# Retention and an MLP on one core: small matmuls in quarters of the array, one stretch for two chunks, and a new order of the head

## The chip, the core and the metric

One NeuronCore of a Trainium2 chip runs one program. The metric is the device time in microseconds (us) of the whole program. TensorE (PE in the profile; PEld are its weight loads) does the matmuls, VectorE (DVE), ScalarE (ACT) and GpSimd (POOL) the element-wise work. SP and POOL issue most of the transfers (DMA). SBUF is the working memory of 128 partitions; matmuls write to PSUM, 8 banks of 512 float32 per partition.

## The reference

q, k and v have shape (8, 8, 576, 64): batch, heads, positions, head width.

```
scores = q @ k.T / sqrt(64)
ret    = scores * D[h]              # D[h][i, j] = gamma_h ** (i - j) for i >= j, else 0
x      = (ret @ v), heads side by side    # 4608 tokens x 512
h      = x @ w_in                   # 512 x 2048
out    = (h * tanh(softplus(h))) @ w_out  # Mish, then 2048 x 512
```

## The kernel before

**Chunks.** Each batch's 576 positions are cut into chunks of 128, the last one of 64; the last ones of two batches share a chunk (c = 4). There are 36 chunks, in `chunks` (L52 to L57): first the eight first chunks (c = 0), then per pair of batches the rest. Four chunks make a tile of 512 tokens, nine tiles in all. Since gamma^(i-j) splits into a factor of i and one of j, a chunk's retention is the causally masked product within the chunk plus q times a running state, the sum of k^T v over earlier chunks.

**Steps of a chunk** (n from 8 on; `N0` = 8):
- `load` (L253): q, k and v by POOL's queue; k is cast to bf16 on the way.
- P (`step_p`, L271, DVE) and V (`step_v`, L276, POOL) scale q and v by the factors of position and head.
- T (`step_t`, L282) transposes q and k: for n < 18 (`NPE`) by eight matmuls against the identity and one ACT copy, later by a transposing transfer on SP's queue (L291).
- S (`step_s`, L294): scores of 8 heads, transposed; a head has 64 rows, so two heads lie in the two row halves of the array (eight pairs of 128-column matmuls), and DVE masks the result into `sm`.
- `state(upto)` (L319) computes at most one more state, if chunk `upto` still lacks its own: eight matmuls add k^T v of one chunk to the PSUM bank `st`; DVE copies it out as `ssb`, doubled in width, with zeros in the half that belongs to the other head (`diag`).
- O (`step_o`, L343): eight matmuls of the state with q and eight of v with `sm`, all with 128 rows and 64 columns of the array, into one bank; DVE copies it to `xT`.

**MLP.** `g1` (L366) makes one of 16 slices of h for a tile: four matmuls over 512 columns into bank `hp`, then Mish on ACT into `gT`. `g2` (L375) does a quarter of 128 output tokens: four matmuls over 512 columns into `ops` (sometimes `hp`); each fourth call readies a result, which `stores` copies (DVE) and SP stores.

**Order.** All orders are written out by hand; each engine and each queue executes its own in order. In the steady loop (L563), tile t runs 16 steps i of g1(t, i) and g2(t-1, i), and a visit of eight steps (w = i % 8) handles two chunks n, n+1 of the next tile: at w = 0 a state if needed and S of n and n+1; at w = 4 a state, O of both, a state; V of n+2, n+3 at w = 0 and 1; T of n+2, n+3 at w = 0, 1 (by TensorE at w = 5, 6, with P at 1, 3); P of n+4, n+5 at w = 7; loads at w = 4, 5. Tile 1's g1 and its first g2 stand in a loop of 24 steps u (L529) in which chunks 8 to 13 come one by one: P and V at u = 4j, S, states and O at 4j + 1, T at 4j + 3.

**Head.** Tile 0 holds the first chunks of batches 0 to 3, which need no state. q comes by SP's queue (L119), the rest by POOL's: k, v of batches 0 and 1 (`load_first_v(0)`, L142), the first quarter of w_in (L143), v of batches 2 and 3 (L144), the other quarters. The v are cast by `f_v` (L220), on POOL for the first three, DVE for the fourth. `f_scores`, `f_out` (L225) do the products; `keep_warm` (L164) issues matmuls on zeros while TensorE would wait. G1 of tile 0 begins with its first four slices on the columns of batches 0 and 1 only (`half`), then, after `f_out` of 2 and 3, on the other columns, and then goes on with whole slices (L495).

**Layout.** Partition 64 e + d of `xT`, group p, holds head 2p + e; w_in's rows (c p) are loaded in the same order, one transfer of 128 partitions for each quarter.

Of the kernel before, what the change touches and what calls it, by code (L numbers as in the profile page):

```python
# [17 lines left out]
def kernel(  # L18
# [63 lines left out]
    w_in_r = moe_w_in.rearrange("(c p) f -> p c f", p=P)  # L82
    w_out_r = moe_w_out.rearrange("(f p) d -> p f d", p=P)

    def load_w_in(f0, n):
        nc.gpsimd.dma_start(out=w_in_t[:, :, ds(f0, n)], in_=w_in_r[:, :, ds(f0, n)])
# [55 lines left out]
    load_first_v(0)  # L142
    load_w_in(0, 512)  # L143
    load_first_v(2)  # L144
# [13 lines left out]

    diag = consts.tile([P, 2], F32)
    nc.vector.memset(diag, 0.0)  # L160
    nc.vector.memset(diag[0:64, 0:1], 1.0)
    nc.vector.memset(diag[64:P, 1:2], 1.0)
# [62 lines left out]
    def f_out(t, b, copy):  # L225
        if b == 0:
            xts[t] = xp.tile([P, KC, NCH * P], BF16, name="xT")
        vb = fst[t]["vb"][b]
        if t == 0:
            pool, name = ((ps_h, "hp"), (ps_h, "hp"), (ps_st, "st"), (ps_o, "ops"))[b]  # L230
            ot = pool.tile([P, NP, P], F32, name=name)
        else:
            ot = ps_sc.tile([P, 2, NP, P], F32, name="sc")[:, 0]
        for p in range(NP):
            for e in range(2):
                nc.tensor.matmul(ot[ds(64 * e, 64), p, :], lhsT=vb[:, 2 * p + e, :],
                                 rhs=fst[t]["sm", b][:, 2 * p + e, :],
                                 start=(p == 0), stop=True, skip_group_check=True)
        copy(xts[t][:, :, ts(b, P)], ot)  # L239
# [54 lines left out]
    def step_s(n):  # L294
        b, c = chunks[n]
        qk = live[n]["qk"]
        sc = ps_sc.tile([P, 2, NP, P], F32, name="sc")
        for p in range(NP):
            for e in range(2):
                r = ds(64 * e, 64)  # L300
                nc.tensor.matmul(sc[:, e, p, :], lhsT=qk[r, 1, p, :], rhs=qk[r, 0, p, :],  # L301
                                 start=True, stop=True)
        sm = tr.tile([P, 2, NP, P], BF16, name="sm", bufs=3)
        m = mask if c < 4 else mask2
        nc.vector.tensor_tensor(  # L305
            sm.rearrange("p e n i -> p (e n) i"), sc.rearrange("p e n i -> p (e n) i"),
            m.unsqueeze(1).to_broadcast([P, 2 * NP, P]), op=OP.mult)
        live[n].update(sc=sc, sm=sm)
# [10 lines left out]
    def state(upto):  # L319
# [11 lines left out]
        for p in range(NP):  # L331
# [3 lines left out]
        ssb = tr.tile([P, 2, NP, 64], BF16, name="ssb", bufs=6)  # L335
        nc.vector.tensor_tensor(  # L336
            ssb.rearrange("p e n d -> p e (n d)"),
            st.rearrange("p n d -> p (n d)").unsqueeze(1).to_broadcast([P, 2, NP * 64]),
            diag.unsqueeze(2).to_broadcast([P, 2, NP * 64]), op=OP.mult)
# [3 lines left out]
    def step_o(n):  # L343
        b, c = chunks[n]
        t, s = divmod(n, NCH)
        assert done[0] > state_of[n]
        qk, vs, sc, sm = (live[n][x] for x in ("qk", "vs", "sc", "sm"))
        ot = ps_o.tile([P, NP, P], F32, name="ops") if t == 2 else sc[:, 0]
        halves = [(0, P, b, c - 1)] if c < 4 else [(0, 64, b, 3), (64, 64, b + 1, 3)]
        for i0, iw, bb, cc in halves:  # L350
            for p in range(NP):
                for e in range(2):
                    nc.tensor.matmul(ot[ds(64 * e, 64), p, ds(i0, iw)], lhsT=st_sb[bb, cc][:, e, p, :],  # L353
                                     rhs=qk[:, 0, p, ds(i0, iw)],
                                     start=(i0 == 0 and p == 0), stop=False, skip_group_check=True)
        for p in range(NP):
            for e in range(2):
                nc.tensor.matmul(ot[ds(64 * e, 64), p, :], lhsT=vs[:, 2 * p + e, :], rhs=sm[:, e, p, :],  # L358
                                 start=False, stop=True, skip_group_check=True)
        if s == 0:  # L360
            xts[t] = xp.tile([P, KC, NCH * P], BF16, name="xT")
        nc.vector.tensor_copy(xts[t][:, :, ts(s, P)], ot)  # L362
# [3 lines left out]
    def g1(t, f, cols=slice(0, NCH * P)):  # L366
# [3 lines left out]
        for c in range(KC):  # L370
            nc.tensor.matmul(hp[:, cols], lhsT=w_in_t[:, c, ts(f, P)], rhs=xts[t][:, c, cols],  # L371
                             start=(c == 0), stop=(c == KC - 1))
        nc.scalar.activation(gts[t][:, f, cols], hp[:, cols], AX.Mish)  # L373

    def g2(t, i):  # L375
# [3 lines left out]
        if part == 0:  # L379
            if (t == nT - 1 and s % 2) or (t == 1 and s < 2):  # L380
# [49 lines left out]
    def att(n, steps):  # L430
        if n >= n_chunks:
            return
        for step in steps:
            {"P": step_p, "V": step_v, "T": step_t, "S": step_s, "O": step_o}[step](n)
# [4 lines left out]
    half = (slice(0, 2 * P), slice(2 * P, 4 * P))  # L439
# [18 lines left out]
    keep_warm(3, ps_h, "hp")  # L458
    f_out(0, 0, dve)
    f_out(0, 1, act)  # L460
    f_scores(0, 1)
    f_v(0, 3, dve)
    keep_warm(3, ps_st, "st")
    for f in range(4):
        g1(0, f, half[0])
    f_out(0, 2, act)
    f_out(0, 3, dve)
    for f in range(4):
        g1(0, f, half[1])
# [25 lines left out]
    for f in range(4, nF):  # L495
        g1(0, f)
# [30 lines left out]

    att(N0, "PV")
    for u in range(24):  # L529
        j, w = divmod(u, 4)  # L530
        if w == 0 and j > 0:
            att(N0 + j, "PV")
# [7 lines left out]
        elif w == 1 and j > 0:  # L540
            if j > 3:
                state(N0 + j - 1)
            if j < 5:
                att(N0 + j - 1, "S")
            if j < 4:
                state(N0 + j - 1)
            if j > 1:
                att(N0 + j - 2, "O")
            if j == 4:
                state(N0 + j - 1)  # L550
            stores()
        elif w == 2 and 0 < j < 5:
            f_state(1, j - 1, nc.vector)
        elif (w == 3 and j < 5) or (w == 2 and j == 5):
            att(N0 + j, "T")
# [6 lines left out]

    for t in range(2, nT + 1):  # L563
        for i in range(nF):
            n, w = NCH * (t + 1) + i // 8 * 2, i % 8
            if t in (3, 4) and i in (4, 12):
                load_k0(2 * t - 2 + i // 8)
            by_pe = n + 2 < NPE
            if w == 0:
                stores()  # L570
                state(n + 1)
                att(n, "S")
                att(n + 1, "S")
            if w == 4:
                state(n + 3)
                stores()
                att(n, "O")
                att(n + 1, "O")
                state(n + 3)
            if by_pe and w in (1, 3):  # L580
                att(n + 2 + w // 2, "P")
            if w in (0, 1):
                att(n + 2 + w, "V")
            if w in (4, 5):
                more_loads(n + w - 2 + PF)
            if w - (5 if by_pe else 0) in (0, 1):
                att(n + 2 + (w == 1 or w == 6), "T")
            if w == 7 and n + 4 >= NPE:
                att(n + 4, "P")
                att(n + 5, "P")  # L590
            stores()
            if t < nT:
                g1(t, i)
            if t == 2:
                if i % 2:
                    g2(1, 8 + i // 2)
            elif t < nT or i < 12:
# [33 lines left out]
```

## Time and profile before

| | us |
|---|---|
| three runs | 312.32, 312.5, 315.58 |
| median | 312.5 |
| the profiled execution, its time | 313.61 |
| its span, first to last instruction | 311.9 |
| TensorE busy / VectorE / ScalarE / GpSimd in that span | 300.3 / 137.1 / 110.7 / 143.6 |
| TensorE busy in 0 to 20 us / 80 to 260 us | 13.7 of 20 / 178.8 of 180 |
| mean of a 512-column matmul from start to modelled end | 0.38 |
| granted TensorE clock | 1.00 |

A line of the timeline gives the start, the time from the first start to the last end, the engine, the source line, the operation, what it writes and reads, the rows * columns of the array that it uses, shape and type of the moving operand, how many instructions are merged, and in brackets how long the engine stood idle ahead of it and what released it. Matmuls overlap: the distance from start to start tells what one costs. In groups, the figures behind the bar are busy us, mean ns of one, idle us ahead of them. 42.85 MB move in the span; the mean busy share of the transfer engines is nine tenths or more in nearly every slice until 160 us.

### The profile page before, as it was taken

What the parts mean: (1) busy time and instruction counts of PE and PEld (TensorE: products, weight loads), DVE (VectorE), ACT (ScalarE), POOL (GpSimd) and SP (SyncE); (2) the same over time, 40 slices, a digit from 0 to 9 for tenths busy, and PEclk for the clock granted to TensorE, in tenths of its full rate; (3) what the DMA queues carried; (4) which work ended last, traced back from release to release, by engine and by line L of the source; (5) the groups of instructions that cost most, each with busy time, mean ns of one, the idle gap of its engine ahead of it and who ended that gap; (6) DMA issues with size and microseconds to landing.
All of it is one profiled execution on the core that took longest, in us unless ns stands there. A gap on an engine that the chain in (4) does not pass through costs nothing.

```text
span 311.9 us, 5809 instructions
## 1 busy us (share of the span) xinstructions
PE 300.3 (96%) x2429; PEld 152.3 (49%) x2468; DVE 137.1 (44%) x200; ACT 110.7 (36%) x183; POOL 143.6 (46%) x178
## 2 busy tenths in 40 slices
PE   7769999999999999999999999999999999999995
PEld 3444554555465554545454444545454544444444
DVE  4723455778637635443434453535354332001111
ACT  4546345671453623233333333232323333333300
POOL 8578849989985976274726262612010000000000
PEclk9999999999999999999999999999999999999999
DMA  7999999999995999999996949371504100010031
GB/s 177 234 206 205 220 208 221 256 171 175 232 203 96 148 181 191 155 195 146 179 178 116 189 88 218 77 144 37 101 36 101 36 34 36 35 34 34 36 101 68
DMA packets 73642, 42.85 MB, mean 137 GB/s; under 512 B 58640, under 2 KB 64528, under 8 KB 73616
## 3 DMA queue, kind: packets, MB, share of 16 engines
q0 software_dynamic: 48640, 27.27, 61.1%
q1 hardware_dynamic: 24832, 15.08, 23.3%
q8 instruction: 19, 0.31, 0.5%
q10 hardware_dynamic: 144, 0.13, 0.1%
q14 instruction: 7, 0.06, 0.1%
HBM read 38.80 MB, written 9.44 MB: 155 GB/s over the span
## 4 chain that ended last, share of the span: by engine, by line
PE 92%; issue 2%; DMA 2%; POOL 2%; DVE 0%; ACT 0%; POOLq 0%; ACTq 0%
PE hp L371 39%; PE ops L386 30%; PE hp L386 4%; PE sc L301 3%; PE st L333 3%; DMA gT<-in_v_dram 2%; PE hp L403 2%; PE sc L353 2%; PE sc L358 2%; PE sc L288 1%; PE st L403 1%; PE ops L403 1%; PE hp L414 1%; POOL gT L106 1%; POOL vb L222 1%
## 5 line engine op out<-in xcount | busy, mean ns | idle before, releaser
L371 PE MATMUL hp<-xT,w_in_t 128*128 128x512 bf16 (+1 forms) x562 | 141.3, 373 | 2.2 <-DVE xT L239 0.8
L373 ACT ACTIVATE gT<-hp 128x512 bf16<-128x512 f32 (+1 forms) x148 | 86.8, 586 | 156.4 <-PE hp L371 144.2
L386 PE MATMUL ops<-w_out_t,gT 128*128 128x512 bf16 x430 | 110.1, 379 | 0.4
L371 PEld LDWEIGHTS <-w_in_t 128*128 128x128 bf16 x592 | 55.1, 98 | 61.9 <-DVE xT L239 1.3
L386 PEld LDWEIGHTS <-gT 128*128 128x128 bf16 x496 | 48.2, 98 | 58.1 <-issue 0.8
L422 DVE COPY res<-ops 128x512 f32<-128x512 f32 x28 | 19.3, 688 | 82.7 <-PE ops L386 79.7
L279 POOL TENSOR_TENSOR vs<-vraw,gv 128x512 bf16<-128x512 f32 x28 | 30.3, 1096 | 51.8 <-PE sc L358 37.6
L336 DVE TENSOR_TENSOR ssb<-st,diag 128x512 bf16<-128x512 f32 x32 | 21.9, 685 | 47.2 <-PE st L333 47.2
L305 DVE TENSOR_TENSOR sm<-sc,mask 128x1024 bf16<-128x1024 f32 x28 | 33.0, 1215 | 6.2 <-PE sc L301 6.2
L263 POOL DMA_DIRECT2D qraw<-in_q_dram x24 | 21.8, 910 | 12.8 <-DVE qks L273 9.6
L263 POOL DMA_DIRECT2D vraw<-in_v_dram x24 | 21.8, 908 | 2.9 <-DMA vpair<-in_v_dram 1.5
L263 POOL DMA_DIRECT2D qks<-in_k_dram x24 | 21.8, 906 | 1.3 <-DMA w_out_t<-in_moe_w_out_dram 0.9
L273 DVE TENSOR_TENSOR qks<-qraw,gq 128x512 bf16<-128x512 f32 x28 | 20.2, 758 | 0.0
L362 DVE CAST xT<-sc 128x512 bf16<-128x512 f32 x24 | 15.3, 680 | 0.0
L386 PE MATMUL hp<-w_out_t,gT 128*128 128x512 bf16 x61 | 14.7, 379 | 0.2
L289 ACT COPY qkT<-sc 128x1024 bf16<-128x1024 bf16 x10 | 10.1, 1010 | 8.0 <-PE sc L288 8.0
L215 DVE TENSOR_TENSOR sm<-sc,dmask 128x1024 bf16<-128x1024 f32 x8 | 9.4, 1220 | 5.0 <-PE sc L211 5.0
L353 PE MATMUL sc<-qkT,ssb 128*64 128x128 bf16 (+1 forms) x224 | 9.5, 213 | 0.0
L358 PE MATMUL sc<-sm,vs 128*64 128x128 bf16 x192 | 9.4, 219 | 0.0
L301 PE MATMUL sc<-qkT 64*128 64x128 bf16 x224 | 9.0, 218 | 0.0
L403 PEld LDWEIGHTS <-gT 128*128 128x128 bf16 x64 | 5.8, 98 | 6.5
L267 POOL DMA_DIRECT2D qraw<-in_q_dram x8 | 5.6, 706 | 7.3 <-DVE qks L273 7.3
(103 smaller groups left out, 192.0 us busy)
## 6 DMA issues: line engine op xcount, KB each, us to landing
out_dram<-res SPq DMA_DIRECT2D x31, 256.0 KB, 3.0
qraw<-in_q_dram POOLq DMA_DIRECT2D x24, 256.0 KB, 6.0
vraw<-in_v_dram POOLq DMA_DIRECT2D x24, 256.0 KB, 6.8
qks<-in_k_dram POOLq DMA_DIRECT2D x24, 128.0 KB, 6.4
w_in_t<-in_moe_w_in_dram POOLq DMA_DIRECT2D x4, 512.0 KB, 11.1
w_out_t<-in_moe_w_out_dram POOLq DMA_DIRECT2D x4, 512.0 KB, 9.8
gT<-in_q_dram SPq DMA_DIRECT2D x4, 256.0 KB, 4.9
gT<-in_k_dram POOLq DMA_DIRECT2D x8, 128.0 KB, 6.3
```

The costliest lines, as they stand in the source:

```text
L263: nc.gpsimd.dma_start(out=t, in_=src[b, :, ds(P * c, P), :].rearrange("h p d -> p h d"))
L273: nc.vector.tensor_tensor(live[n]["qks"][:, 0], live[n]["q"], gq[:, c, :].unsqueeze(2).to_broadcast([P, H, D]), op=OP.mult)
L279: nc.gpsimd.tensor_tensor(vs, live[n]["v"], gv[:, c, :].unsqueeze(2).to_broadcast([P, H, D]), op=OP.mult)
L301: nc.tensor.matmul(sc[:, e, p, :], lhsT=qk[r, 1, p, :], rhs=qk[r, 0, p, :], start=True, stop=True)
L305: nc.vector.tensor_tensor(sm.rearrange("p e n i -> p (e n) i"), sc.rearrange("p e n i -> p (e n) i"), m.unsqueeze(1).to_broadcast([P, 2 * ...
L336: nc.vector.tensor_tensor(ssb.rearrange("p e n d -> p e (n d)"), st.rearrange("p n d -> p (n d)").unsqueeze(1).to_broadcast([P, 2, NP * 64 ...
L353: nc.tensor.matmul(ot[ds(64 * e, 64), p, ds(i0, iw)], lhsT=st_sb[bb, cc][:, e, p, :], rhs=qk[:, 0, p, ds(i0, iw)], start=(i0 == 0 and p == ...
L371: nc.tensor.matmul(hp[:, cols], lhsT=w_in_t[:, c, ts(f, P)], rhs=xts[t][:, c, cols], start=(c == 0), stop=(c == KC - 1))
L373: nc.scalar.activation(gts[t][:, f, cols], hp[:, cols], AX.Mish)
L386: nc.tensor.matmul(ops, lhsT=gts[t][:, f, ts(s, P)], rhs=w_out_t[:, f, :], start=(f == 0), stop=(f == nF - 1))
L403: nc.tensor.matmul(outs[0, s], lhsT=gts[0][:, f, ts(s, P)], rhs=w_out_t[:, f, :], start=(f == 0), stop=(f == nF - 1))
L422: copy(ot, ops)
```

## The change

It has six parts.

1. Heads h and h + 4 now share a group of `xT`: partition 64 a + r of group c holds head 4a + c. w_in is loaded in that order of rows, each quarter by two transfers of 64 partitions.
2. The state is copied out as it is, without the zeros, 256 elements per partition instead of 512; in the steady loop (`two`) half by DVE, half by ACT. Its product with q (`outputs_end`) uses quarters of the array, 64 rows by 64 columns, as does S now: twice as many matmuls with half the columns.
3. O becomes `outputs` and `outputs_end` for two chunks at once, into two banks, copied to `xT` by ACT and DVE. `visit` puts state, outputs, state, outputs_end and S of the next two chunks in one stretch, at w = 6.
4. In the steady loop P moves to w = 4, 5, transposing transfers to w = 7 and the next w = 0, T on TensorE to w = 2, 4; two g1 stand together at w = 0 and 4.
5. `hold`: at w = 4 POOL copies one element of each of the two transposed chunks, so that it waits for their transfers before it issues its next loads.
6. In the head, v of batches 2 and 3 is loaded ahead of w_in; the half-width G1 is gone, and G1 starts whole after the four `f_out`; other engines take some of the copies, and the counts of `keep_warm` change. In the loop over u, P, V and T get their own lists, S and O stand at u = 9, 15 and 22.

```diff
-    w_in_r = moe_w_in.rearrange("(c p) f -> p c f", p=P)
+    w_in_r = moe_w_in.rearrange("(a c r) f -> a r c f", a=2, r=64)
-        nc.gpsimd.dma_start(out=w_in_t[:, :, ds(f0, n)], in_=w_in_r[:, :, ds(f0, n)])
+        for a in range(2):
+            nc.gpsimd.dma_start(out=w_in_t[ds(64 * a, 64), :, ds(f0, n)], in_=w_in_r[a, :, :, ds(f0, n)])
...
     load_first_v(0)
+    load_first_v(2)
     load_w_in(0, 512)
-    load_first_v(2)
...
@@ step_s
-                r = ds(64 * e, 64)
-                nc.tensor.matmul(sc[:, e, p, :], lhsT=qk[r, 1, p, :], rhs=qk[r, 0, p, :],
-                                 start=True, stop=True)
+                for a in range(2):
+                    r, j = ds(64 * e, 64), ds(64 * a, 64)
+                    nc.tensor.matmul(sc[j, e, p, :], lhsT=qk[r, 1, p, j], rhs=qk[r, 0, p, :],
+                                     start=True, stop=True, skip_group_check=True)
...
@@ state
-        ssb = tr.tile([P, 2, NP, 64], BF16, name="ssb", bufs=6)
-        nc.vector.tensor_tensor(
...
+        ssb = tr.tile([P, NP, 64], BF16, name="ssb", bufs=6)
+        if two:
+            nc.vector.tensor_copy(ssb[:, 0:2, :], st[:, 0:2, :])
+            nc.scalar.copy(ssb[:, 2:NP, :], st[:, 2:NP, :])
+        else:
+            nc.vector.tensor_copy(ssb, st)
...
+    def outputs(n, banks):
+        both = [pool.tile([P, 2, 2 * P], F32, name=name) for pool, name in banks]
+        for x in range(2):
+            sm, vs = live[n + x]["sm"], live[n + x]["vs"]
+            for h in range(NP):
+                for a in range(2):
+                    hh = NP * a + h
+                    nc.tensor.matmul(both[h % 2][ds(64 * a, 64), h // 2, ts(x, P)], lhsT=vs[:, hh, :],
+                                     rhs=sm[:, hh % 2, hh // 2, :],
+                                     start=(x == 0 and h < 2), stop=False, skip_group_check=True)
+        return both
...
+    def outputs_end(n, both):
...
+                        e, p = h % 2, (NP * a + h) // 2
+                        r = ds(64 * e, 64)
+                        nc.tensor.matmul(both[e][ds(64 * a, 64), h // 2, ds(P * x + i0, iw)],
+                                         lhsT=st_sb[bb, cc][r, p, :], rhs=qk[r, 0, p, ds(i0, iw)],
+                                         start=False, stop=True, skip_group_check=True)
...
+        for e, copy in enumerate((nc.scalar.copy, nc.vector.tensor_copy)):
+            copy(xts[t].rearrange("p (h e) i -> p e h i", e=2)[:, e, :, ds(P * s, 2 * P)], both[e])
...
+    def hold(n):
+        nc.gpsimd.tensor_copy(held[:, n % 2:n % 2 + 1], live[n]["qk"][:, 1, NP - 1, P - 1:P])
+
+    def visit(n, banks, upto, two=False):
+        state(upto, two)
+        both = outputs(n, banks)
+        state(upto, two)
+        outputs_end(n, both)
+        for m in (n + 2, n + 3):
+            att(m, "S")
...
@@ head
-    keep_warm(3, ps_h, "hp")
-    f_out(0, 0, dve)
+    keep_warm(4, ps_h, "hp")
+    f_scores(0, 1)
+    f_out(0, 0, act)
     f_out(0, 1, act)
-    f_scores(0, 1)
-    f_v(0, 3, dve)
-    keep_warm(3, ps_st, "st")
-    for f in range(4):
-        g1(0, f, half[0])
-    f_out(0, 2, act)
-    f_out(0, 3, dve)
-    for f in range(4):
-        g1(0, f, half[1])
+    keep_warm(6, ps_st, "st")
+    f_v(0, 3, act)
+    f_out(0, 2, dve)
+    f_out(0, 3, act)
+    keep_warm(2, ps_sc, "sc")
...
@@ loop over u
+    pv = {0: 0, 4: 1, 8: 2, 11: 3, 16: 4, 18: 5}
+    tp = {3: 0, 6: 1, 11: 2, 13: 3, 18: 4, 20: 5}
...
+        if u == 9:
+            state(N0 + 1)
+            att(N0, "S")
+            att(N0 + 1, "S")
+            state(N0 + 1)
+        elif u == 15:
+            visit(N0, ((ps_o, "ops"), (ps_h, "hp")), N0 + 3)
+            state(N0 + 3)
+        elif u == 22:
+            visit(N0 + 2, ((ps_h, "hp"), (ps_h, "hp")), N0 + 5)
...
@@ steady loop
+            if w == 6 and n < n_chunks:
+                visit(n, ((ps_h, "hp"), (ps_h, "hp")), min(n + 4, last), True)
                 state(n + 3)
...
+            if w in (4, 5) and n + 4 >= NPE:
+                att(n + w, "P")
...
+            if w == 4 and NPE <= n + 2 < n_chunks:
+                hold(n + 2)
+                hold(n + 3)
...
+            if w in (2, 4) and n + 2 < NPE:
+                att(n + 1 + w // 2, "T")
             if w == 7 and n + 4 >= NPE:
-                att(n + 4, "P")
-                att(n + 5, "P")
+                att(n + 4, "T")
+            if w == 0 and n + 2 >= NPE:
+                att(n + 3, "T")
```

## The prediction

> **What bounds the kernel now.** I read the page first (shares of the engines, the chain that ended last), then TensorE's timeline, stretch by stretch, then the timeline of the first 35 us, then the groups by form and the landings of the transfers. The page says which engine counts:
>
> ```profile
> span 311.9 us, 5809 instructions
> PE 300.3 (96%) x2429; PEld 152.3 (49%) x2468; DVE 137.1 (44%) x200; ACT 110.7 (36%) x183; POOL 143.6 (46%) x178
> ...
> PE 92%; issue 2%; DMA 2%; POOL 2%; DVE 0%; ACT 0%; POOLq 0%; ACTq 0%
> ```
>
> Nothing but TensorE carries the chain, so only what TensorE executes, or waits for, can move the end. Its timeline in the steady part, one visit of two chunks (16.02 us from one S stretch, 203.04, to the next, 219.06):
>
> ```profile
> 202.08 1.03 PE L386 MATMUL ops<-w_out_t,gT 128*128 128x512 bf16 x4
> 203.04 0.62 PE L301 MATMUL sc<-qkT 64*128 64x128 bf16 x16
> ...
> 204.46 1.03 PE L386 MATMUL ops<-w_out_t,gT 128*128 128x512 bf16 x4
> ...
> 209.64 1.03 PE L386 MATMUL ops<-w_out_t,gT 128*128 128x512 bf16 x4
> 210.60 0.32 PE L333 MATMUL st<-vs,qks 128*64 128x64 bf16 x8
> 210.75 0.42 PE L353 MATMUL sc<-qkT,ssb 128*64 128x64 bf16 x16
> 211.00 0.39 PE L358 MATMUL sc<-sm,vs 128*64 128x128 bf16 x8
> 211.23 0.39 PE L353 MATMUL sc<-qkT,ssb 128*64 128x128 bf16 x8
> 211.45 0.39 PE L358 MATMUL sc<-sm,vs 128*64 128x128 bf16 x8
> 211.80 0.32 PE L333 MATMUL st<-vs,qks 128*64 128x64 bf16 x8
> ...
> 212.92 1.03 PE L386 MATMUL ops<-w_out_t,gT 128*128 128x512 bf16 x4
> ```
>
> Read the starts; the durations overlap. A group of four 512-column matmuls takes 0.865 us, 0.216 each. From that: the S stretch is due at 202.08 + 0.865 = 202.945, starts 0.09 late, and the next group (0.865 before 204.46) starts at 203.595. So S is 0.65 = 0.09 to enter, 0.45 for 16 matmuls (eight pairs, one per row half), 0.10 to leave. The O stretch is due at 210.505 and over at 212.055: 1.55 = 0.09 + state 0.15 + four groups of eight in column halves (0.25 where the chunk is split, else 0.223 each) + a wait of 0.13 + state 0.15 + 0.10. The 0.13 wait: the state bank may only be written again when DVE's copy of it (0.69, start 0.24 after the last matmul's start) is through. Where a state stands ahead of S it costs 0.25, 0.10 of it for the change from column halves to row halves.
>
> ```profile
> L336 DVE TENSOR_TENSOR ssb<-st,diag 128x512 bf16<-128x512 f32 x32 | 21.9, 685 | 47.2 <-PE st L333 47.2
> L417 DVE COPY half<-hp 128x256 f32<-128x256 f32 x1 | 0.4, 424 | 2.8 <-PE hp L414 2.8
> ```
>
> Summed the same way over the trace: tile 1 (55 to 77 us) has five stretches, 0.67 + 1.12 + 1.12 + 1.44 + 0.79 = 5.1; after it twelve S (12 x 0.65, four with a state: + 4 x 0.25) 8.8 and twelve O (seven of 1.54, four of 1.44, one of 1.14) 17.7. Together 31.6 us; everything else after 20 us is 512-column matmuls (and transposes, which stay). The head:
>
> ```profile
> 7.12 1.17 POOL L117 DMA_DIRECT2D gT<-in_v_dram  x1
> ...
> 14.77 2.11 PE L371 MATMUL hp<-xT,w_in_t 128*128 128x256 bf16 x16
> ...
> 17.67 0.87 POOL L222 CAST vb<-gT 128x512 bf16<-128x512 f32 x1 [4.51 <-DMA gT<-in_v_dram]
> ...
> 18.60 0.41 PE L236 MATMUL st<-sm,vb 128*64 128x128 bf16 x8 [1.72 <-POOL vb L222]
> ...
> 20.03 12.67 PE L371 MATMUL hp<-xT,w_in_t 128*128 128x256 bf16 x63 [0.79 <-DVE xT L239]
> ...
> 32.53 0.61 PE L194 MATMUL sc<-ident,qbx 128*128 128x128 bf16 x8
> ```
>
> The second pair of v lands at 17.6 and G1 of the second half waits for it. G1 is over at 32.53. The half-width matmuls take 2.11 / 16 = 0.132 each where half of 0.216 would be 0.108.
>
> **The change, part by part.** Base: this execution, 313.61 us (span 311.9, 1.7 around it); it is 1.1 above the median of 312.5, and gains are carried to the median.
>
> *Quarters and one stretch.* A visit now runs: enter 0.09; state 0.15; sm.v of both chunks, 16 matmuls in column halves, 8 x 0.056 = 0.45; state 0.15; change of mode 0.10; state.q, 16 matmuls of 64 x 64, four quads; S of the next two chunks, 32 matmuls of 64 x 64, eight quads; leave 0.10. No row shows four quarters side by side. From below, a quad can't beat one 128-column step, 0.056 (the pair's). From above, it is two pair steps, 0.112. Between lies the rate of issue: 16 matmuls, each with its weights, in 0.25 us (210.75 to 211.00) is 0.0156 each, 0.063 a quad. Row halves and column halves both run a pair in one step, so I take the near row: 0.056, that is 0.22 and 0.45.
>
> The skill's page "TensorE: Matmul & The Clock Gate" (section "Wait — 56ns, not 53.3ns?") says that starts never come closer than about 25 ns. The 0.0156 above is already below it; by the rule 48 matmuls would take 1.2 us instead of 0.67, 0.5 a visit, some 7 us in all, and the change would lose.
>
> *The wait between the two states.* The diagonal mask goes, so the copy has 256 elements, and in the steady part half each on DVE and ACT. DVE at 512 takes 0.688 (res copy), at 256 0.424, so 128 takes about 0.29. It starts 0.24 after the last state matmul's start and frees the bank 0.14 later (211.65 to 211.80): 0.67, covered by 0.03 + 0.45. A wait of 0.19 stays, 0.11 where a new batch begins (there the row shows 0.06 to restart). So the old wait does not vanish, it grows a little, as less work stands between. Bounds: 0 and, with DVE's undivided 0.424, 0.33.
>
> *Sum of the stretches.* A visit: 1.71 + 0.19 = 1.90. Eleven with two states and S: 11 x 1.71 + 7 x 0.19 + 4 x 0.11 = 20.6; three of them need a third state after S: 3 x 0.25; the last has neither state nor S: 0.95. That is 22.3 against 26.5. Tile 1 has three stretches: u = 9 (state, S, S, state) 1.2, u = 15 2.25, u = 22 2.0: 5.45 against 5.1, since S of two more chunks falls in it. Net 31.6 - 27.75 = 3.9 us gained; with 0.063 a quad 3.2; with no wait left 5.6.
>
> *What moves to other engines.* xT of a pair is one copy on ACT (0.585) and one on DVE (0.69) instead of two on DVE; ACT also gets 22 half states. Per visit ACT is busy 4.8 of 16 us, DVE 7.2; neither is near. The copies free the two hp banks while S and the following g2 (0.45 + 0.865) run, so g1 finds a bank. In t >= 3 two g2 groups (1.7 us) stand before the visit and cover the Mish (0.60) that must free them. In tile 1 and t = 2, P stands a step ahead of T, with DVE's two sm (1.22 each) before it: T(14) comes 4.3 us after the visit, DVE needs about 3.9; close, priced at nothing.
>
> *Transposing transfers.* P and T move earlier, but S more: T to S shrinks from 15.4 and 13.6 us to 12.1 and 10.4 (seven and six steps of 1.73). The transfers land in 9.4 to 11.8 us in the first three visits (108 to 143 us, all queues full), in 3.1 to 6.9 later. So only visits 16 to 20 are at stake. `hold` makes POOL wait for them ahead of load_k0 and the loads: 18 copies of at most 0.29 (L486's row), and behind them wait six loads that nobody reads for two visits. With fewer loads beside them they should land in under 9.4. Bounds: nothing, and 3 x 4.8 = 14 (a first issue of 5.1 on SP, the longest of the rows, puts the second off by 3.4: 11.8 + 3.4 - 10.4). I take 0.5: the first has no hold ahead of it. On SP, T stands ahead of the stores, which have four buffers.
>
> *Head.* v(2) is issued at 6.4, ahead of w_in 0, so it takes the place that w_in 0 had: lands at 14.1 to 15. w_in 0 then lands when the same bytes had come, 17.0 to 17.6. Eight half issues of 0.525 (L106) to 0.756 (L86) instead of four: POOL is through w_in at 12.8 to 14.2 rather than 11.84, and the v casts behind it (0.58 each) end at 14.9 to 16.0. TensorE then has six warming matmuls (1.3) and f_out 2 and 3; with the copy (0.24 + 0.69) G1 may start at 16.6 to 18.1. I take 17.7, just behind w_in 0. 64 x 0.216 = 13.8 ends it at 31.5: 1.0 gained (0.4 to 1.6). The later w_in land at 19.8 to 24.9, each before its turn (21.2 on). From there the loads' order is the same; v of tile 1 lands at 45.06, and its products, at 48.3 instead of 49.4, still cover that.
>
> "DMA: Bandwidth & Descriptors" (section "Rules for kernel authors") says of two transfers to disjoint partition halves that they serialize, so one whole transfer is better: by it the split is pure cost. Here the layout needs it, and its issue time is above.
>
> *Sum.* 3.9 + 1.0 - 0.5 = 4.4. This execution would go to 309.2, the median to **308.1**.
>
> **Rivals.**
> - *Quads run as pairs.* 12 more steps of 0.056 a visit, 0.67, on thirteen visits, and as many for the last one's state.q and the S of u = 9 together: 14 x 0.67 = 9.4 in all, 317.5, slower. For it: no quad in this trace. Against it: either split alone runs side by side with starts 3.4 ns apart. It decides from about 0.082 a quad on, where the 4.4 are gone. A limit on dispatch would look the same: a visit has 80 matmuls where the longest stretch of before has 56.
> - *Transposes late.* Visits 16, 18 and 20 wait 1.4 each or more: from 312 up, 318 at worst likely. For it: 11.8 landed against 10.4 lead. Against: hold, and the landings of 3 to 7 us once loads are few. It costs the gain from 1.5 a visit on.
> - *The state's wait grows.* If DVE or ACT is not free when the state ends (a store's copy of 0.69 ahead of it), the wait is 0.5 rather than 0.19: 11 x 0.35 = 3.9, 312.0: nothing gained but the head. Against: DVE stood idle 4.86 us ahead of L336.
>
> **How the numbers follow.** Forecast 0.64 (own range 305.0 to 310.5: no wait left and the best head, 308.1 - 1.7 - 0.6 = 305.8, some more for the wait taken for T; 0.063 a quad and the worst head, 309.4, some more for T); pairs 0.13; late transposes 0.12; state's wait 0.08; something else 0.03. 1% of the time, 3.1 us, is about what a measurement tells from nothing, so the bounds are 309.4 and 315.6. Faster: 0.58 of the forecast's and 0.03 of others, 0.61; slower: the pairs, and 0.05 of late transposes and the rest, 0.18; within: 0.21. The range reaches from 305.0 to 313.5, up to the state's wait and most of the late transposes; beyond it are the pairs.
>
> **What would show it.** Right: one stretch of about 1.9 us each 15.7 us on TensorE, with L301's successor taking 0.056 for four; G1 starting at 17.7 and over at 31.5; a wait of about 0.2 ahead of the second state. Wrong: 32 S matmuls in 0.9 us; TensorE waiting for the transposing transfer at visits 16 to 20; G1 waiting for xT or w_in past 18.5.

## The result, and the profile after

| | before | after |
|---|---|---|
| median of the runs (four of each) | 312.52 | 317.52 |
| lowest to highest | 312.32 to 315.58 | 317.40 to 317.67 |
| profiled execution, its span | 313.61, 311.9 | 317.57, 315.9 |
| TensorE: S, state and O stretches from 55 us on | 31.6 | 31.8 |
| G1 of tile 0 over at | 32.53 | 35.18 |

The changed kernel is slower: ratio 1.0146, 95% interval 1.0101 to 1.0190. The forecast was 308.1, its range ended at 313.5.

The page of the changed kernel, to be laid beside the three lines shown of before (TensorE is 96% busy in both):

```profile
span 315.9 us, 6341 instructions
PE 301.7 (96%) x2682; PEld 150.7 (48%) x2682; DVE 118.8 (38%) x181; ACT 124.2 (39%) x217; POOL 149.0 (47%) x200
...
PEclk9979999999999999999999999999999999999999
...
PE 89%; DVE 3%; DMA 3%; POOL 2%; issue 1%; ACT 1%; DVEq 0%; POOLq 0%; ACTq 0%
```

Two things are new. The clock row (one digit for each fortieth of the span, in tenths) has a 7 in its third slice, about 16 to 24 us. And the chain that ended last now runs through VectorE (3%) and ScalarE (1%), which held 0% of it before.

The timeline of one visit, all engines (16.02 us to the next visit, as before):

```profile
202.13 0.32 PE L330 MATMUL st<-vs,qks 128*64 128x64 bf16 x8
...
202.27 0.62 PE L352 MATMUL hp<-sm,vs 128*64 128x128 bf16 x16
...
202.55 0.29 DVE L334 CAST ssb<-st 128x128 bf16<-128x128 f32 x1 [2.48 <-PE st L330]
...
202.88 0.27 ACT L335 CAST ssb<-st 128x128 bf16<-128x128 f32 x1 [1.77 <-DVE ssb L334]
...
203.19 0.32 PE L330 MATMUL st<-v0s,k 128*64 128x64 bf16 x8 [0.30 <-ACT ssb L335]
...
203.44 0.42 PE L369 MATMUL hp<-qkT,ssb 64*64 64x128 bf16 x16
...
203.69 0.62 PE L298 MATMUL sc<-qkT 64*64 64x128 bf16 x32
...
204.24 1.04 PE L414 MATMUL ops<-w_out_t,gT 128*128 128x512 bf16 x4
```

The two half copies do not run side by side. ScalarE had stood idle for 1.77 us, and what released it at 202.88 was VectorE's half. Only behind it may the second state start. From the starts: sm.v is issued through at 202.27 + 0.45 = 202.72, the second state starts at 203.19, so the wait is 0.47. The bracket says 0.30 because it counts from the modelled end. The quarters do what they should: 32 S matmuls in 204.24 - 0.10 - 203.69 = 0.45, and state.q's 16 in 0.25.

The head, from the timeline of 4 to 23 us:

```profile
14.79 0.62 POOL L87 DMA_DIRECT2D w_in_t<-in_moe_w_in_dram  x1 [1.66 <-DMA gT<-in_v_dram]
...
15.39 1.73 POOL L218 CAST vb<-gT 128x512 bf16<-128x512 f32 x3
...
16.08 0.96 PE L232 MATMUL hp<-sm,vb 128*64 128x128 bf16 x16 [2.84 <-POOL vb L218]
...
16.98 2.68 PE L163 MATMUL st<-zeros 128*128 128x512 bf16 x6
...
21.37 1.89 PE L399 MATMUL hp<-xT,w_in_t 128*128 128x512 bf16 x8
```

POOL's last issue of w_in waited 1.66 us until v of batches 2 and 3 had landed. The casts queued behind it therefore began at 15.39 (11.99 before), TensorE stood idle for 2.84 us, and the six warming matmuls took 2.68 us, where six take 1.47 at full clock (in the run with more warming matmuls below): the granted clock is 0.54 in 17 to 18 us, 0.50 from 18 to 20, and 1.00 from 21 on. G1 starts at 21.37 and is over at 35.18. The halved clock is no accident of this one execution: the four runs have mean granted clocks of 0.995, 0.995, 0.995 and 0.989, and 3.4 or 6.8 us at half clock take 0.005 or 0.011 off the mean of 316 us.

And tile 1, where one transpose was late:

```profile
71.92 2.35 DVE L302 TENSOR_TENSOR sm<-sc,mask 128x1024 bf16<-128x1024 f32 x2
...
74.52 1.82 DVE L269 TENSOR_TENSOR qks<-qraw,gq 128x512 bf16<-128x512 f32 x2
...
75.79 0.62 PE L284 MATMUL sc<-ident,qks 128*128 128x128 bf16 x8 [1.23 <-DVE qks L269]
```

T of chunk 12 was due at 74.40 and waited 1.40 us for P: VectorE had two sm and a state copy of the visit ahead of it, and the first P took 1.21 us (the second 0.68). While it ran, GpSimd ran V (74.12 to 75.17) and a transfer's issue. Over all the traces, the 159 P that had no GpSimd instruction beside them took at most 0.69 us; the longest of all, 2.94, had one beside it.

### The profile page after: what moved, and what is told of

Read it like the earlier page. It is cut to its first block, busy times and chain, and to the rows that moved or that the text cites. A ratio compares the mean times of both kernels' runs of the same rounds, so it can differ in the third digit from the quotient of the medians.

```text
span 315.9 us, 6341 instructions
## 1 busy us (share of the span) xinstructions
PE 301.7 (96%) x2682; PEld 150.7 (48%) x2682; DVE 118.8 (38%) x181; ACT 124.2 (39%) x217; POOL 149.0 (47%) x200
## 4 chain that ended last, share of the span: by engine, by line
PE 89%; DVE 3%; DMA 3%; POOL 2%; issue 1%; ACT 1%; DVEq 0%; POOLq 0%; ACTq 0%
PE hp L399 39%; PE ops L414 31%; PE st L330 3%; PE hp L414 3%; DMA gT<-in_v_dram 3%; PE hp L431 2%; PE sc L298 2%; PE sc L284 1%; PE hp L369 1%; PE st L431 1%; PE ops L431 1%; PE hp L442 1%; DVE ssb L334 1%; ACT ssb L335 1%; PE st L163 1%
## 5 line engine op out<-in xcount | busy, mean ns | idle before, releaser
L399 PE MATMUL hp<-xT,w_in_t 128*128 128x512 bf16 x576 | 136.6, 379 | 0.1
L401 ACT ACTIVATE gT<-hp 128x512 bf16<-128x512 f32 x144 | 86.1, 598 | 112.2 <-PE hp L399 112.2
L414 PEld LDWEIGHTS <-gT 128*128 128x128 bf16 x496 | 47.4, 98 | 56.0
L259 POOL DMA_DIRECT2D qraw<-in_q_dram x24 | 21.8, 907 | 3.6 <-DMA vpair<-in_v_dram 1.5
L334 DVE CAST ssb<-st 128x128 bf16<-128x128 f32 x22 | 6.4, 292 | 43.2 <-PE st L330 43.2
L335 ACT CAST ssb<-st 128x128 bf16<-128x128 f32 x22 | 5.9, 266 | 26.6 <-DVE ssb L334 26.6
L375 DVE CAST xT<-hp 128x512 bf16<-128x512 f32 x14 | 9.7, 692 | 4.5 <-PE hp L369 3.9
L330 PE MATMUL st<-vs,qks 128*64 128x64 bf16 x192 | 7.6, 200 | 2.6 <-ACT ssb L335 2.5
L330 PEld LDWEIGHTS <-qks 128*64 128x64 bf16 x192 | 5.1, 110 | 9.3 <-issue 7.6
L375 ACT CAST xT<-hp 128x512 bf16<-128x512 f32 x13 | 7.7, 591 | 4.2 <-PE hp L369 4.2
```

The source lines that it names most:

```text
L259: nc.gpsimd.dma_start(out=t, in_=src[b, :, ds(P * c, P), :].rearrange("h p d -> p h d"))
L330: nc.tensor.matmul(st[ds(64 * e, 64), p, :], lhsT=ks[:, 2 * p + e, :], rhs=vs[:, 2 * p + e, :], start=(c == 0 and p == 0), stop=True, skip ...
L375: copy(xts[t].rearrange("p (h e) i -> p e h i", e=2)[:, e, :, ds(P * s, 2 * P)], both[e])
L399: nc.tensor.matmul(hp, lhsT=w_in_t[:, c, ts(f, P)], rhs=xts[t][:, c, :], start=(c == 0), stop=(c == KC - 1))
L401: nc.scalar.activation(gts[t][:, f, :], hp, AX.Mish)
L414: nc.tensor.matmul(ops, lhsT=gts[t][:, f, ts(s, P)], rhs=w_out_t[:, f, :], start=(f == 0), stop=(f == nF - 1))
```

## The experiments

The theory after the result: G1 ends 2.65 us later, T of chunk 12 waits 1.40, the stretches gained nothing (+0.2), a small wait of G2 went (-0.2); together the 4.0 us of span. Its rival is the one that I had named and that hit the time, quads that run as pairs. The other questions: why does ScalarE's half wait, what holds POOL, and does `hold` do anything? Times without an interval are of one execution, and the changed kernel was not run again beside them; so what an edit did is read from its own stretch, and the time comes second.

### The visit

**One copy of the state** instead of two halves:

```diff
-                visit(n, ((ps_h, "hp"), (ps_h, "hp")), min(n + 4, last), True)
+                visit(n, ((ps_h, "hp"), (ps_h, "hp")), min(n + 4, last))
```

> The changed kernel, but every state is copied out by DVE alone (one copy of 256 elements). Theory (the second state waits for DVE's 0.29 and ACT's 0.27 one after the other): the copy takes 0.42, the second state follows the first after 0.92 instead of 1.06, a visit costs 2.05 instead of 2.20, eleven visits 1.5 to 1.8 us, time about 315.9. Rival (quads run as pairs and the visit is bound by TensorE): nothing changes, 317.5.

317.19. Visits of two states took 1.97 to 2.08 us (2.13 to 2.31 in the changed kernel), those of three 2.22 (2.50 to 2.57). One undivided copy of 0.42 is faster than two halves in a row, 0.16 to 0.28 a visit, as the theory had it. The time hides this: G1 started at 22.28, and in one visit S waited for a transposing transfer:

```profile
172.25 0.42 PE L298 MATMUL sc<-qkT 64*64 64x128 bf16 x16 [0.98 <-DMA qkT<-qks]
```

**Two tiles for the copy**, in case the tile that both halves write ties them:

```diff
-        ssb = tr.tile([P, NP, 64], BF16, name="ssb", bufs=6)
+        ssb = tr.tile([P, 2, 64], BF16, name="ssb", bufs=6)
+        ssc = tr.tile([P, 2, 64], BF16, name="ssc", bufs=6)
...
+        nc.vector.tensor_copy(ssb, st[:, 0:2, :])
+        (nc.scalar.copy if two else nc.vector.tensor_copy)(ssc, st[:, 2:NP, :])
...
```

> The changed kernel, but the two halves of a copied state are tiles of their own. If ACT waits for DVE because both write one tile, the two copies run side by side, the wait ahead of the second state falls from 0.47 to about 0.2 and eleven visits gain 0.27 each: about 314.5. If ACT waits because both read one PSUM bank, ACT still starts behind DVE and the time stays at 317.5.

319.79, and the visits of two states stay at 2.13 to 2.31. (The 2.2 us more than the changed kernel lie ahead of the steady loop: G1 was over 1.3 later, and two T of tile 1 waited 1.2 and 0.9.) A visit of its timeline:

```profile
204.76 0.29 DVE L334 CAST ssb<-st 128x128 bf16<-128x128 f32 x1 [2.48 <-PE st L330]
...
205.08 0.27 ACT L335 CAST ssc<-st 128x128 bf16<-128x128 f32 x1 [1.77 <-DVE ssb L334]
...
205.40 0.32 PE L330 MATMUL st<-v0s,k 128*64 128x64 bf16 x8 [0.30 <-ACT ssc L335]
```

ScalarE now writes a tile of its own and still starts when VectorE is through. So it is not the written tile. The changed kernel itself has the other half of this comparison, the two copies to `xT`, which write one tile and read two banks:

```profile
203.94 0.69 DVE L375 CAST xT<-hp 128x512 bf16<-128x512 f32 x1
204.09 0.59 ACT L375 CAST xT<-hp 128x512 bf16<-128x512 f32 x1
```

These do run side by side. What the halves of the state have in common is the bank `st` that both read. The Trainium skill's page "PSUM — Partial Sum Buffer" (section "PSUM bank collisions raise a hardware error") says that ScalarE and VectorE may not access one bank on the same partitions at once, two reads included, and that a scheduler therefore puts one behind the other. These rows agree (0.29, then 0.27). A state in two banks, or halves by partitions, was not tried, so that the bank, and not some other tie in the program, sets the one behind the other is argued and not shown.

**The second state behind S**, except in visits that need three states, where two stay ahead:

```diff
+        three = n + 3 < n_chunks and state_of[n + 3] - done[0] >= 1
+        if three:
+            state(upto, two)
         outputs_end(n, both)
         for m in (n + 2, n + 3):
             att(m, "S")
+        if not three:
+            state(upto, two)
```

> The changed kernel, but the second state of a visit stands behind S (in three visits, which need a third state, it stays where it was). Theory: the wait of 0.47 goes, one more change of mode comes (0.10), eight visits of the steady loop and the one at u = 22 cost about 1.85 instead of 2.20: 9 x 0.35 = 3.2, about 314.3. Rival (the visit is bound by the matmuls themselves): the order is of no account, or 0.1 a visit is lost, 317.5 to 318.5.

317.04. A visit of TensorE's timeline:

```profile
186.80 0.32 PE L330 MATMUL st<-vs,qks 128*64 128x64 bf16 x8
...
187.74 0.62 PE L298 MATMUL sc<-qkT 64*64 64x128 bf16 x32
188.29 0.32 PE L330 MATMUL st<-vs,qks 128*64 128x64 bf16 x8
188.54 1.04 PE L418 MATMUL ops<-w_out_t,gT 128*128 128x512 bf16 x4
```

S stands where the wait was. A visit takes 1.83 to 1.84 us instead of 2.13 to 2.31 (one took 2.12: its S waited 0.25 for a transposing transfer), and the stretches take 28.8 us together, 3.0 less. The end moved only 0.5. The head of this execution was 1.1 us later still (G1 at 22.51), the same T waited 0.86, and a new wait came twice:

```profile
94.94 2.35 DVE L302 TENSOR_TENSOR sm<-sc,mask 128x1024 bf16<-128x1024 f32 x2
...
97.52 0.27 ACT L335 CAST ssb<-st 128x128 bf16<-128x128 f32 x1 [2.71 <-DVE ssb L334]
97.68 1.09 ACT L405 ACTIVATE gT<-hp 128x512 bf16<-128x512 f32 x2
...
98.34 1.02 PE L403 MATMUL hp<-xT,w_in_t 128*128 128x512 bf16 x4 [0.76 <-ACT gT L405]
```

The state's copy now stands behind both sm on VectorE, ScalarE's half behind VectorE's, and the Mish that must free G1's bank behind that. From start to start it cost 0.92 and 0.86 us. In the kernels below with one copy by VectorE this wait does not come.

**S in pairs**, 16 matmuls by row halves as before the change:

```diff
-                for a in range(2):
-                    r, j = ds(64 * e, 64), ds(64 * a, 64)
-                    nc.tensor.matmul(sc[j, e, p, :], lhsT=qk[r, 1, p, j], rhs=qk[r, 0, p, :],
-                                     start=True, stop=True, skip_group_check=True)
+                r = ds(64 * e, 64)
+                nc.tensor.matmul(sc[:, e, p, :], lhsT=qk[r, 1, p, :], rhs=qk[r, 0, p, :],
+                                 start=True, stop=True)
```

> The changed kernel, but S is 16 matmuls in row halves as before, for 32 in quarters. Theory (four quarters run side by side, 0.056 for four): S takes 0.45 either way, a change of mode of 0.1 comes in each of 13 visits: about 318.8. Rival (quads run as pairs): S in quarters costs 0.45 more than S in halves, so this gains 0.35 a visit, about 313.

319.55, with G1 at 22.64. From one visit to the next it is 16.13 us instead of 16.02: 0.11 for the added change of mode is lost, and nothing is won back. The rival would have had it no slower there. It falls: four quarters do run side by side.

### The head

**The kernel before, each quarter of w_in as two transfers** of 64 partitions, and nothing else:

```diff
-        nc.gpsimd.dma_start(out=w_in_t[:, :, ds(f0, n)], in_=w_in_r[:, :, ds(f0, n)])
+        for a in range(2):
+            nc.gpsimd.dma_start(out=w_in_t[ds(64 * a, 64), :, ds(f0, n)], in_=w_in_r[ds(64 * a, 64), :, ds(f0, n)])
```

> The kernel before, with each quarter of w_in loaded by two transfers of 64 partitions and nothing else changed. Theory (only eight transfers of POOL's queue may be under way, so the split, not the order, stops POOL): the eighth half waits until the first half transfers have landed, about 14.1, the casts of v start at about 14.8 instead of 12.0, and the first products and the half-width G1 come 2.5 to 3 us later; since v of batches 2 and 3 lands at 17.6 all the same, the whole G1 ends 0 to 2 us later: 312.5 to 315. Rival (only the issue time counts, 2 us more of POOL): casts at about 14, no wait, 312.5 to 313.

The casts begin at 14.46 instead of 11.99, the clock is halved from 15.1 to 18.6, and G1 ends at 34.49 instead of 32.53, 2.0 us later. (315.58 as a whole, and 316.05 for the one execution of before beside it, which lies at the top of that kernel's runs, 312.3 to 316.2; so here the end of G1 is the measure, not the end of the kernel; that execution's mean clock was 0.989.) POOL's queue says why:

```profile
12.66 0.61 POOL L87 DMA_DIRECT2D w_in_t<-in_moe_w_in_dram  x1 [0.80 <-DMA gT<-in_v_dram]
13.85 0.61 POOL L87 DMA_DIRECT2D w_in_t<-in_moe_w_in_dram  x1 [0.57 <-DMA w_in_t<-in_moe_w_in_dram]
14.46 1.17 POOL L223 CAST vb<-gT 128x512 bf16<-128x512 f32 x2
```

These are POOL's 13th and 14th transfers; the first waits for the 5th to land, the second for the 6th. In the changed kernel, too, it is the 14th that waited for the 6th, v of batches 2 and 3. A transfer waited for the one eight places ahead of it. It holds for the whole queue: in all 18 traces, with 128 to 132 transfers of POOL's queue each, none was issued before the one eight ahead had landed, while 17 to 38 in each were issued before the one seven ahead had. Splitting four transfers into eight used up the places.

**The last quarter of w_in issued behind the casts:**

```diff
-    for i in range(1, 4):
+    for i in range(1, 3):
         load_w_in(512 * i, 512)
...
+    load_w_in(512 * 3, 512)
```

> The changed kernel, but POOL issues the last quarter of w_in behind the three casts of v instead of ahead of them. Theory (POOL's eighth half transfer of w_in waits until v of batches 2 and 3 has landed, at 14.8, and the casts wait behind it; TensorE's clock then drops to half): the casts start at about 12.6, the clock stays at 1.0, G1 starts when the second half of w_in 0 has landed, about 18.3 instead of 21.4, time 314.0 to 315.0. Rival (G1 is late because w_in 0 lands late): G1 starts as before at 21, 317.5.

315.5. The two lines of the head that matter:

```profile
12.98 1.17 POOL L218 CAST vb<-gT 128x512 bf16<-128x512 f32 x2 [0.44 <-DMA gT<-in_v_dram]
...
18.70 1.67 PE L399 MATMUL hp<-xT,w_in_t 128*128 128x512 bf16 x7 [0.28 <-DMA w_in_t<-in_moe_w_in_dram]
```

The casts come 2.4 us earlier, the clock stays at 1.00, and G1 runs from 18.70 to 32.51: as in before, but not ahead of it, since w_in 0 itself landed only at some 18.5. Of these 2.67 us only 2.0 reached the end: P was late for three T, 0.61, 0.86 and 0.48 us.

**Twelve more warming matmuls** behind the second scores, casts left late:

```diff
     f_scores(0, 1)
+    keep_warm(12, ps_h, "hp")
```

> The changed kernel with 12 more warming matmuls behind f_scores of the second pair, in the time in which TensorE waits for the casts. Theory (the wait of 2.8 us lets the clock fall to half for 3.4 us or more): the clock stays at 1.0, the six warming matmuls take 1.3 instead of 2.7, G1 starts at about 20.0 instead of 21.4: about 316.2. Rival (the late casts alone): G1 at 21.4, 317.5.

319.41. The head did what was expected: full clock, the six warming matmuls in 1.47 us, G1 at 19.76. So the halved clock, and not only the idle time, cost the head 1.6 us. The page "TensorE: Matmul & The Clock Gate" (section "What's actually happening") has the clock fall after an idle window of about 3.4 us; here an idle stretch of 2.84 was enough. But the gain was given back: the first P of T(12) took 2.01 us, T waited 2.2, the clock was halved once more from 76.3 to 79.7, behind an idle stretch of 2.03, and one S waited 0.77 for a transposing transfer.

### P and T in tile 1

**P two steps earlier**:

```diff
-    pv = {0: 0, 4: 1, 8: 2, 11: 3, 16: 4, 18: 5}
+    pv = {0: 0, 4: 1, 8: 2, 11: 3, 14: 4, 18: 5}
```

> The changed kernel, but P and V of chunk 12 stand at u = 14, ahead of the visit of u = 15, instead of at u = 16. Theory (TensorE's transposes of u = 18 wait 1.4 us for P, which stands on DVE behind two score masks and three copies of the visit): the wait goes, time about 316.1. Rival (P waits for q to land): the wait stays or moves to DVE ahead of the visit, 317.5 or above.

316.53, 1.0 less than the changed kernel. T no longer waits (1.40) and G1 starts 0.48 earlier, but one visit gives some back: S waited 0.63 us in it for a transposing transfer.

### The transfers and `hold`

**Without `hold`:**

```diff
-                hold(n + 2)
-                hold(n + 3)
+                pass
```

> The changed kernel without the two copies by which POOL waits for the transposing transfers. Theory (TensorE never waits for these transfers, with or without): they land later, up to 12 us after issue, with 10.4 us of lead at the least, so visits 16 to 20 may wait 0 to 2 us each; 317.5 to 321. Rival (hold costs time by holding up the loads): 316 to 317.

317.38; the transfers landed in 3.0, 4.5 and 10.5 us (least, median, most) instead of 3.1, 8.1 and 12.3, and S waited in neither. So here they landed sooner without `hold`, against the theory.

**The order of the head alone**, put into the kernel before: v ahead of w_in, w_in in whole transfers, G1 whole, the old stretches and no `hold`:

```diff
+    load_first_v(2)
     load_w_in(0, 512)
-    load_first_v(2)
...
-    keep_warm(3, ps_h, "hp")
-    f_out(0, 0, dve)
+    keep_warm(4, ps_h, "hp")
+    f_scores(0, 1)
+    f_out(0, 0, act)
     f_out(0, 1, act)
-    f_scores(0, 1)
-    f_v(0, 3, dve)
-    keep_warm(3, ps_st, "st")
-    for f in range(4):
-        g1(0, f, half[0])
-    f_out(0, 2, act)
-    f_out(0, 3, dve)
-    for f in range(4):
-        g1(0, f, half[1])
+    keep_warm(6, ps_st, "st")
+    f_v(0, 3, act)
+    f_out(0, 2, dve)
+    f_out(0, 3, act)
+    keep_warm(2, ps_sc, "sc")
...
-    for f in range(4, nF):
+    for f in range(nF):
         g1(0, f)
```

> The kernel before with the head's new order alone: both v ahead of w_in, whole G1, the new places of f_scores, f_out and keep_warm, but each quarter of w_in still one transfer. Theory (the split, not the order, made the head late): POOL does not wait for v, the casts start at about 12.6, the clock stays, G1 starts when w_in 0 has landed, 17.5 to 18.7, and ends at 31.4 to 32.5 against 32.53 before: 0 to 1 us gained on a run of before with a full clock, 311.5 to 312.5. Rival (the order itself is bad): G1 starts at 20 or later and the time is 315 or more.

318.92. G1 runs from 17.51 to 31.34, 1.2 us ahead of before, just as the prediction had the head. And the end is 5.6 us later than that of before beside it (313.32):

```profile
121.59 0.40 PE L301 MATMUL sc<-qkT 64*128 64x128 bf16 x8
126.66 0.41 PE L301 MATMUL sc<-qkT 64*128 64x128 bf16 x8 [4.68 <-DMA qkT<-qks]
```

S of the second chunk waits 4.68 us for its transposing transfer; the first four transfers land here in 14.2 to 18.0 us where none took more than 11.8 in before, and the clock is halved behind it (126.9 to 130.3). The same kernel again, four executions:

> The head-only kernel again, by rounds. Theory: the stall in the second S stretch behind 120 us recurs in most runs, 315 to 319, since the loads reach the queue 1 us or more earlier than in before; by chance in some only, then the runs spread from 311.5 to 319.

319.06, 319.11, 323.5 and 324.98 (median 321.3); the ratio without the longest is 1.024, 1.0152 to 1.0328. The trace kept is that of the longest: landings up to 22.5, S waits 7.5 in all. And with `hold` added to it:

```diff
+            if w == 4 and NPE <= n + 2 < n_chunks:
+                hold(n + 2)
+                hold(n + 3)
```

> The head-only kernel of before with hold added (w = 4, ahead of its loads). Theory (its loss was one late transposing transfer, beside loads that ran ahead of it): transfers land in under 10 us, no S waits, the 1.2 us of the head stay: 311 to 312. Rival (the loss has another cause): 315 to 319 as without hold.

311.49 (311.41 to 312.02), ratio 0.9943, 0.9912 to 0.9974. All transfers land in 2.7 to 5.7 us and S waits for none. With the old stretches the time fell by 7.6 us from the two shortest executions without `hold`, and by more from the others. Of the 7.5 us between the two traces (318.92 and 311.42), 4.86 are S's wait (from start to start), 1.7 the halved clock behind it, and 1.0 an earlier G1 (16.56), where no `hold` stands. In the changed kernel `hold` did nothing to be seen. Why the transfers are late in the one and not in the other is not settled: the queues' order is the same, only the times at which loads meet them differ.

### All mends together

Second state behind S, one copy, last w_in behind the casts (the edits above), and P earlier:

```diff
-    pv = {0: 0, 4: 1, 8: 2, 11: 3, 16: 4, 18: 5}
+    pv = {0: 0, 4: 1, 8: 2, 9: 3, 14: 4, 18: 5}
```

> The changed kernel with what the single runs point to: the second state behind S, state copies by DVE alone, the last quarter of w_in behind the casts, P of chunks 11 and 12 earlier (u = 9 and 14). Theory: 3.5 (states) + 2.7 (head) + 1.4 to 2 (P) off 317.5, 0.8 more for the third states, less what the transposing transfers then make TensorE wait: 309 to 311, below both kernels. Rival (the gains come back as other waits): 312 or more.

310.16 (309.87 to 311.9), ratio 0.9896, 0.9844 to 0.9948. One stretch, at u = 9, now took 2.37 us instead of 1.18, for its state waited behind P. Then both transposes of a pair at w = 7:

```diff
             if w == 7 and n + 4 >= NPE:
                 att(n + 4, "T")
-            if w == 0 and n + 2 >= NPE:
-                att(n + 3, "T")
+                att(n + 5, "T")
```

> The same as c1, but both transposing transfers of a visit are issued right behind the visit before (w = 7), 1.7 us earlier for the second. Theory (a faster visit leaves the second transfer too little lead, as one visit of e1 and one of e5 waited about 1 us for it): such waits go, 0 to 2 us below c1. Rival: the two transfers one upon the other hold up SP's stores, no gain or a loss of up to 1 us.

310.04 (309.95 to 310.11), ratio 0.9879, 0.9826 to 0.9932. Then P of chunk 11 back at u = 11 (`9: 3` becomes `11: 3`):

> c2 with P and V of chunk 11 back at u = 11. Theory (at u = 9, P of chunk 11 waited on DVE for q to land and the state's copy stood behind it, so TensorE waited 1.2 us): the stretch of u = 9 is 1.18 again, T of chunk 11 waits 0 to 0.6 us: 308.9 to 309.5. Rival (the wait at u = 9 is the load of v or k): no change, 310.0.

309.9 (309.51 to 310.32), ratio 0.9901, 0.9873 to 0.9930, against 313.25 of before beside it. The stretch is back at 1.18 (2.22 in the kernel before this one), but two T wait 0.3 us each that did not wait there, so that 0.3 of the 1.0 us reached the end of the profiled executions. What is left in the head is G1's wait for w_in 0, here as in the kernel before this one (1.77):

```profile
18.47 1.89 PE L403 MATMUL hp<-xT,w_in_t 128*128 128x512 bf16 x8 [1.70 <-DMA w_in_t<-in_moe_w_in_dram]
```

And the last one without `hold`, by the edit above:

> c3 without the copies by which POOL waits for the transposing transfers. Theory (the loads beside them make these transfers late by chance): some S stretches wait 1 to 5 us in some runs, median 0 to 3 us above c3 and a wider spread. Rival (hold does nothing): the same as c3.

309.85 (309.39 to 311.13), ratio 0.9905, 0.9872 to 0.9937: no difference. All four lie about 1% below the kernel before and over 2% below the changed one (measured at another time), and are not to be told apart.

## Why the prediction was wrong

Its sum for the profiled execution was 309.2, measured 317.57, 8.4 us more. By its own terms:

| step | forecast | measured | missed by |
|---|---|---|---|
| stretches | 27.75 | 31.8 | +4.05 |
| G1 of tile 0 over at | 31.5 | 35.18 | +3.65 |
| T of chunk 12 waits | 0 | 1.40 | +1.40 |
| transposing transfers | 0.5 | 0 | -0.5 |

That is 8.6; a wait of G2 that went takes off 0.2.

- **"So 128 takes about 0.29 ... A wait of 0.19 stays": this step failed.** The durations were right (0.29 and 0.27). That the two run side by side was taken as given, and no row of before shows two engines reading one bank at once. They ran in a row; the wait was 0.47. That is the size of the rival "the state's wait grows" (0.5), but not its cause: neither engine was late (VectorE had been idle for 2.48 us, ScalarE for 1.77), one waited for the other. Eight visits of two states took 2.23 on the mean (1.87 by the forecast's terms), three of three states 2.52 (2.12): 8 x 0.36 + 3 x 0.40 = 4.1, of which the wait is 0.3 a visit. With the wait covered (state behind S) a visit takes 1.83, under the forecast's 1.90.
- **"Quads 0.056": right.** 0.45 for eight quads, 0.25 for the four of state.q with the change of mode apart. The rival with pairs came out at the measured time, 317.5 against 317.52, and its mechanism is false: the nearness of a sum proves nothing about its terms.
- **"POOL is through w_in at 12.8 to 14.2": this step failed.** The added issues were counted by their own duration, not by what each must wait for; POOL was through at 15.39. The rule on splits that I had weighed ("pure cost") spoke rightly here, but its price is not the issue time: 2.0 us in the kernel before. From there two followers were missing in the working, the idle TensorE and its halved clock (1.6). With the issue moved G1 was over at 31.83 to 33.12 in five runs, with w_in whole at 30.37, 31.34 and 32.02 in three (before: 32.53, forecast: 31.5). So v ahead of w_in is worth about the forecast's 1.0, within a scatter of 1.7, and the split takes most of it back.
- **"T(14) ... close, priced at nothing": mis-sized, and at another chunk.** T(12) in tile 1 had less room, and its P took 1.21, in one run 2.01, instead of 0.68.
- **Transposing transfers: the worry was right, the sign of their risk was not seen whole.** In the changed kernel they cost nothing in the profiled run, 0.25 to 1.0 in four variants of it. In the kernel with the old stretches, which has more lead, they cost 4.7 in one trace and 7.5 in another, and the halved clock behind them more. That a head 1.2 us earlier brings this on is what the runs suggest; how it does so stays open.

Put right, the terms do add up. In the mended kernel with P of chunk 11 back at u = 11 the stretches take 27.7, the forecast's 27.75, though by another order, with the second state behind S; G1 is over at 32.28, 0.8 late; two T wait 0.66 together; the transposing transfers cost nothing where 0.5 was set down. From the forecast's span of 309.2 - 1.7 = 307.5 that makes 308.4, measured 308.1.

## What to carry to other kernels

Before a copy is halved between two engines, look in the trace for two engines that read the same bank at the same time; if there is no such row, price them in a row, and look for work that can stand between the copy and the next write instead. A split transfer is paid in places on its queue: count which earlier transfer must have landed before the added one may be issued, and what waits behind it. Where several waits lie close to the path, a mend in one place moves the loads and may be eaten elsewhere, so a mend is judged by its own stretch first, and by the end only when the others are mended too.

## What the runs showed that I had not expected

- A transfer on POOL's queue waited for the one eight ahead of it (13th for 5th, 14th for 6th).
- TensorE idle for 2.84 us had its clock halved for 3.4 us; in five variants of the changed kernel, with idle stretches of 2.68 to 3.64 in the head, it was halved for 6.8. Idle stretches of up to 1.77 left the clock at 1.00.
- A P on VectorE took from 0.68 to 2.94 us, the longer ones beside work on GpSimd.
- A transposing transfer landed after 2.7 to 22.5 us, among kernels with nearly the same loads.
